# Order of a tile's interleaved Strassen units, its x sums and one h sum, in a fused attention and SiLU MLP kernel

## Chip, cores, metric

The kernel runs on one core of a Trainium2 chip. The metric is the device time of one launch in microseconds (us), the median of several runs; lower is better.

## The reference

Eight batches of eight heads of attention, 576 queries by 64, with keys and values averaged over groups of eight (72 pooled rows), then an MLP without bias on all 4608 tokens:

```python
k_p = k.reshape(B, H, Sp, 8, D).mean(axis=3)        # Sp = 72
v_p = v.reshape(B, H, Sp, 8, D).mean(axis=3)
scores = np.matmul(q, k_p.transpose(0, 1, 3, 2)) / np.sqrt(D)
attn = np.exp(scores - scores.max(-1, keepdims=True)); attn /= attn.sum(-1, keepdims=True)
x = np.matmul(attn, v_p).transpose(0, 2, 1, 3).reshape(4608, 512)
h = x @ w_in                                        # 512 -> 2048
out = (h * sigmoid(h)) @ w_out                      # 2048 -> 512
```

## The kernel before, in words

**Tiles and stages.** The 4608 tokens are cut into nine tiles of 512, numbered 0 to 8 (`NT = 9`, `B = 8`). A tile has an *up* stage (`up`: h = silu(x @ w_in), written to `h_T` as 16 groups of 128 hidden columns) and a *down* stage (`down_quarters`: h @ w_out). While tile t runs, the attention of batch t + 1 is computed between its matmuls; it writes x, transposed, to `xT`. For tiles 7 and 8 there is no attention left to put in.

**Units.** A part of each stage is done by Strassen's scheme: the two operands are cut into 2 by 2 quarters, and seven products of quarter sums take the place of eight. In `up`, a unit covers four groups of hidden columns: unit B the groups 4 to 7, C 8 to 11, A 12 to 15. Its products are numbered 1 to 7, each of four matmuls of 256 columns. Product 2 opens the PSUM bank P, 5 opens Q, 1 opens R; 4 and 7 are added onto P, 3 and 6 onto Q. The readers of these banks use one buffer each, shared by all units: after 2, ScalarE copies P to `r_sb` (L504); after 5, VectorE adds Q and `r_sb` into `rr_sb` (L507); after 1, VectorE forms `t_sb` (L510); after 4 and 3, ScalarE takes the SiLU of P and Q (L495); after 7 and 6, VectorE adds `t_sb` to P and Q into `c_sb` 0 and 1 (L519, L522), of which `h` and `s` take the SiLU on ScalarE. Groups 0 to 3 are plain products of four matmuls of 512 columns (`plain`, L547), with a SiLU each (L553); they are called g0 to g3 below.

**Order of tiles 7 and 8.** It is written out by hand in the two strings of `THREE`, one for each tile: `A4` is product 4 of unit A, `Ah` its first SiLU, `g1` plain group 1. The engines execute in program order.

**Sums.** Five of the seven products of a unit take a sum or difference of two x quarters, `x_sum` (`unit_x_sum`, L454, on VectorE), made once for a tile and used by its three units. In the same way the down stage's products 2, 5, 1, 7 and 6 take sums of `h_T` quarters, `h_sum` (`hidden_sum`, L615, on VectorE), made in halves of 1024 columns (7 in one piece of 2048).

**When sums are issued.** `up` and `down_quarters` walk through numbered steps (58 in the up stage of tiles 7 and 8, one per plain matmul and two per product; 112 in a down stage, one per matmul). A list of fillers holds pairs of a step and a function; `spread` issues a filler after the matmul of its step. Two fillers of one list with one step keep the order in which they were added. So a step number is a place in the program and sets the order on each engine, not a time.

In the down stage of tile 6 the fillers at steps 97 and 101 multiply the numerators of batch 7 (second and third visit, 192 columns each) into `xT` (L403); the filler at 103 makes tile 7's x sums. Tile 7 reads the first 64 tokens of batch 7 and so only its first visit, written at step 56.

**Down stage.** Product order is 2 and 5 (second halves of the contraction first), 1, 4, 3, 7, 6, in the banks P, Q, R, with readers L668 to L690. In the last tile, 8, products 1 to 6 are done first for 128 tokens of each half (steps 32 to 71), then for the other 128 (steps 72 to 111), so that stores start earlier; there L677 (copy of P after product 4) and L682 (copy of Q after product 3) are VectorE copies. Product 6 of the first pass takes steps 64 to 71. Product 7 is added onto P after L677 has read it, and 6 onto Q after L682 has read it.

```python
for n in (2, 5):
    h_at = {B - 1: 54, B: 50}.get(t, 36 if t > 1 else 45)
    f_up.append((h_at, lambda n=n: hidden_sum(n, 4, 8)))
...
product(3, 0, KQ, cc)
nc.vector.tensor_copy(out=o_sb[0][:, cs, HI], in_=ps["Q"][:, cs])
```

Of the kernel before, what the change touches and what calls it, by code (L numbers as in the profile page):

```python
# [36 lines left out]
def kernel(  # L37
# [11 lines left out]
    B, H, S, D = q.shape  # L49
# [274 lines left out]
    def part(g, f):  # L324
        return ((g, f * QF, (f + 1) * QF),)
# [36 lines left out]
    def denominators(b, segs, on_dve=False):  # L362
        st = batches[b]
        w = width(segs)
        es = st["es", segs]
        den_ps = ps_tile([128, 512], FP32, "at", "den_ps")
        for s in range(4):
            nc.tensor.matmul(  # L368
                den_ps[32 * s : 32 * (s + 1), :w],
                lhsT=ones, rhs=es[:, s, :], start=True, stop=True,  # L370
            )
        rec = mid.tile([128, VW], FP32, tag="rec", bufs=4, name="rec")[:, :w]
        if on_dve:
            nc.vector.reciprocal(rec, den_ps[:, :w])
        else:
            lnd = mid.tile([128, VW], FP32, tag="lnd", name="lnd")[:, :w]
            nc.scalar.activation(lnd, den_ps[:, :w], func=AF.Ln)  # L377
            nc.scalar.activation(rec, lnd, func=AF.Exp, scale=-1.0)
        st["rec", segs] = rec

    def numerators(b, segs, tags=("at", "at")):
        st = batches[b]
        w = width(segs)
        g0, i0, i1 = segs[0]
        c0 = b * S % NX + i0 * QP
        cols = slice(c0, c0 + (i1 - i0) * QP)
        es = st.pop(("es", segs))
        rec = st.pop(("rec", segs))
        nu = []
        for c in range(2):  # L390
            nu_ps = ps_tile([128, 512], FP32, tags[c], "nu_ps")
            for g, _, _, cs in seg_cols(segs):
                for s in range(4):
                    nc.tensor.matmul(  # L394
                        nu_ps[32 * s : 32 * (s + 1), cs],
                        lhsT=st["vp"][:, 4 * g + s, c::2],
                        rhs=es[:, s, cs],
                        start=True, stop=True,
                    )
            nu.append(nu_ps)  # L400
        ng = len(segs)
        for c in range(2):
            nc.vector.tensor_mul(  # L403
                out=xT[:, 2 * g0 + c : 2 * (g0 + ng - 1) + c + 1 : 2, cols],
                in0=nu[c][:, :w].rearrange("r (g n) -> r g n", g=ng),
                in1=rec.rearrange("r (g n) -> r g n", g=ng),
            )
# [33 lines left out]
    def x_quarter(t, i, j):  # L441
        c0 = (t * NTT + j * NQ) % NX
        return xT[:, 2 * i : 2 * i + 2, c0 : c0 + NQ]
# [8 lines left out]
    def unit_x_sum(t, n):  # L452
        a, b = U_X[n]
        nc.vector.tensor_tensor(  # L454
            out=x_sum[:, U_XI[n]], in0=x_quarter(t, *a), in1=x_quarter(t, *b),
            op=ALU.subtract if n in (3, 4) else ALU.add,
        )
# [143 lines left out]
    def quarter(i, j, ks):  # L601
        return h_T[:, j * KQ + ks.start : j * KQ + ks.stop, i * NQ : (i + 1) * NQ]
# [9 lines left out]
    def hidden_sum(n, k0, k1):  # L612
        a, b, op = H_SUMS[n]
        ks = slice(k0, k1)
        nc.vector.tensor_tensor(  # L615
            out=h_sum[n][:, ks, :], in0=quarter(*a, ks), in1=quarter(*b, ks), op=op
        )
# [175 lines left out]
    def load_half_2(name, half):  # L793
# [1 line left out]
            load_slots(nc.gpsimd, 2, name, i0, i1, half)  # L795

    THREE = (
        "g0 A2 A5 g1 A4 B2 A3 A1 B5 A7 C2 A6 B4 B3 B1 C5 Ah B7 As C4 Bh B6 C1 C3 C7 Bs"
        " g2 C6 Ch Cs g3",
        "A2 A5 g0 A4 B2 A3 A1 B5 A7 C2 A6 B4 B3 B1 C5 Ah B7 As C4 Bh B6 C1 C3 C7 Bs g1"  # L800
        " C6 Ch Cs g2 g3",
    )
# [1 line left out]
    for t in range(NT):  # L804
        a = t + 1
        f_up, f_down = [], []
        if t == 0:
            GA = 11
            items = [(g, 0, HS) for g in range(GA)]
            items += [(g, HS, NTT - HS) for g in range(GA)]  # L810
            items += [(g, 0, NTT) for g in range(GA, KG)]
            f_up += [(1, lambda: denominators(0, part(0, 1), on_dve=True))]
            f_up += [(5, lambda: denominators(0, part(1, 1), on_dve=True))]
            f_up += [(13, lambda: numerators(0, part(0, 1)))]
            f_up += [(17, lambda: numerators(0, part(1, 1)))]
        else:
            G = lambda *gs: [(g, 0, NTT) for g in gs]
            if t == 1:
                items = (
                    G(12, 13, 14, 15) + [(0, "251")] + G(8) + [(0, "43")] + G(9)  # L820
                    + [(0, "7h6")] + G(10) + [(0, "s")] + G(11, 0, 1, 2, 3)
                )
            elif t >= B - 1:
                items = []
                for it in THREE[t - B + 1].split():
                    items += [(("BCA".index(it[0])), it[1])] if it[0] in "ABC" else G(int(it[1]))
            else:
                items = (
                    G(12, 13) + [(0, "251")] + G(14) + [(0, "43")] + G(15) + [(0, "76")]
                    + [(1, "2")] + [(0, "hs")] + [(1, "51")] + G(0) + [(1, "43")] + G(1)  # L830
                    + [(1, "7h6")] + G(2) + [(1, "s")] + G(3)
                )
            if t < B - 1:
                for n in U_X:
                    f_up.append((0, lambda n=n: unit_x_sum(t, n)))
# [3 lines that stand above are left out]
            f_up.append((56, lambda: hidden_sum(6, 4, 8)))  # L839
            for n, k0 in ((2, 0), (5, 0), (1, 4), (1, 0)):  # L840
                f_up.append((64, lambda n=n, k0=k0: hidden_sum(n, k0, k0 + 4)))
            f_down.append((33, lambda: hidden_sum(7, 0, 8)))
            f_down.append((71, lambda: hidden_sum(6, 0, 4)))

        for n, t0, f_to, at, parts in (
            (1, 0, f_down, 48, (0, PW)), (3, 0, f_down, 52, (0, PW)),
# [61 lines left out]
                    f_down.append((nu_at[n], lambda: numerators(a - 1, visits[2])))  # L908
        if t in (B - 2, B - 1):
            for n in (4, 1, 3, 7, 6):  # L910
                f_down.append((103 if t < B - 1 else 44, lambda n=n: unit_x_sum(t + 1, n)))
        if t == B - 2:
            k_w = big.tile([128, 4, 2, 256], BF16, tag="k_raw2", name="w_sum12")
            v_w = big.tile([128, 4, 2, 256], BF16, tag="v_raw2", name="w_sum12")
# [37 lines left out]
```

The softmax here doesn't subtract the row's maximum and nothing guards it: scores larger than these inputs give would overflow.

## Time and profile before

| what | us |
|---|---|
| median of 5 runs (lowest, highest) | 284.66 (284.32, 284.85) |
| the profiled execution's own time | 284.85 |
| its span in the profile | 283.0 |
| around the span | 1.85 |
| TensorE matmul busy | 276.5 (98%) |
| VectorE busy | 232.3 (82%) |
| ScalarE busy | 184.5 (65%) |
| up stage of tile 7, first matmul to first matmul of its down stage | 228.92 to 242.30 |
| down stage of tile 7 | 242.30 to 254.66 |
| up stage of tile 8 | 254.66 to 267.28 |
| down stage of tile 8, to the end of the last VectorE addition | 267.28 to 280.32 |

Busy time counts a matmul from its start to its modelled end, so successive matmuls overlap by some 0.16 us; stage lengths are taken between starts. The rest of the span after 280.32 is the last store. PE is TensorE's matmuls, PEld its weight loads, DVE is VectorE, ACT ScalarE, SP and POOL the two other queues. "Chain" is the chain of waits that ended last, followed back from the last instruction.

### The profile page before, as it was taken

The numbers are of one execution on the slowest core, as the hardware profiler recorded it, in microseconds if no ns is written. First come the engines' busy times: TensorE is split into PE (matmuls) and PEld (weight loads), VectorE is DVE, ScalarE is ACT, GpSimd is POOL, SyncE is SP. The second block draws the span as 40 slices with busy tenths as digits, with TensorE's granted clock in tenths as the row PEclk, the third lists the DMA queues.
The fourth block names the chain that finished last, engine by engine and source line by source line (L and its number), as shares of the span: only waits on it lengthen the run. The fifth ranks groups of instructions, "written<-read, shape, count | busy, mean of one in ns | idle before, by whom it ended". The sixth has DMA issues, their size and how long they took to land.

```text
span 283.0 us, 6989 instructions
## 1 busy us (share of the span) xinstructions
PE 276.5 (98%) x2823; PEld 198.2 (70%) x2823; DVE 232.3 (82%) x418; ACT 184.5 (65%) x361; POOL 61.4 (22%) x79
## 2 busy tenths in 40 slices
PE   8889999999999999999999999999999999999995
PEld 5348544456777677767888776687667778688784
DVE  4887846899978898879896998799888978966973
ACT  1677766568567876687668857885779477326800
POOL 8655216332140214021402130441100000000001
PEclk9999999999999999999999999999999999999999
DMA  7999999896749863995498439597830032004104
GB/s 216 273 262 231 213 309 169 220 182 118 144 55 202 163 139 50 188 204 109 77 194 178 89 82 179 138 142 110 131 104 0 2 94 56 2 0 123 29 2 148
DMA packets 31312, 37.70 MB, mean 133 GB/s; under 512 B 10352, under 2 KB 22256, under 8 KB 31280
## 3 DMA queue, kind: packets, MB, share of 16 engines
q0 software_dynamic: 23920, 27.03, 53.2%
q1 hardware_dynamic: 6928, 9.58, 12.2%
q10 hardware_dynamic: 432, 0.66, 0.8%
q8 instruction: 22, 0.36, 0.5%
q14 instruction: 10, 0.08, 0.1%
HBM read 36.70 MB, written 9.44 MB: 163 GB/s over the span
## 4 chain that ended last, share of the span: by engine, by line
PE 90%; DVE 5%; DMA 2%; ACT 1%; issue 1%; DVEq 0%
PE hp_ps L547 23%; PE o_psP L655 15%; PE o_psQ L655 15%; PE u_psP L487 7%; PE u_psQ L487 7%; PE o_psR L655 5%; PE sc_ps L350 4%; PE o_ps L582 3%; PE nu_ps L394 3%; PE u_psR L487 2%; PE den_ps L368 2%; DMA raw<-in_k_dram 2%; PE warm_ps L704 1%; DVE w_sum L633 1%; ACT es L358 1%
## 5 line engine op out<-in xcount | busy, mean ns | idle before, releaser
L547 PE MATMUL hp_ps<-xT,w_in_sb 128*128 128x512 bf16 (+3 forms) x380 | 74.7, 337 | 0.1
L655 PEld LDWEIGHTS <-h_sum 128*128 128x128 bf16 x640 | 60.5, 98 | 12.8 <-DVE h_sum L615 1.9
L553 ACT ACTIVATE h_T<-hp_ps 128x512 bf16<-128x512 f32 (+2 forms) x87 | 46.5, 541 | 19.0 <-PE hp_ps L547 16.9
L615 DVE TENSOR_TENSOR h_sum<-h_T 128x1024 bf16<-128x1024 bf16 (+1 forms) x72 | 50.5, 742 | 5.0 <-ACT h_T L553 5.0
L547 PEld LDWEIGHTS <-w_in_sb 128*128 128x128 bf16 x380 | 36.2, 98 | 21.6 <-issue 0.6
L358 ACT ACTIVATE es<-sc_ps 72x384 bf16<-72x384 f32 (+1 forms) x100 | 38.9, 468 | 10.3 <-PE sc_ps L350 10.2
L487 PEld LDWEIGHTS <-w_sum 128*128 128x128 bf16 x340 | 33.3, 98 | 7.5
L655 PEld LDWEIGHTS <-h_T 128*128 128x128 bf16 x256 | 24.1, 98 | 4.4 <-issue 0.9
L403 DVE TENSOR_TENSOR xT<-nu_ps,rec 128x384 bf16<-128x384 f32 (+1 forms) x50 | 23.9, 530 | 0.2
L495 ACT ACTIVATE h_T<-c_sb 128x512 bf16<-128x512 f32 x34 | 20.6, 626 | 5.2 <-DVE c_sb L519 5.0
L377 ACT ACTIVATE lnd<-den_ps 128x384 f32<-128x384 f32 (+1 forms) x23 | 11.1, 484 | 19.4 <-PE den_ps L368 19.4
L158 DVE STREAM_TRANSPOSE qT<-q_bf 128x576 bf16<-128x576 bf16 x32 | 23.0, 753 | 0.6 <-DMA q_bf<-in_q_dram 0.6
L273 DVE TENSOR_TENSOR raw<-raw 128x384 f32<-128x384 f32 (+3 forms) x20 | 12.3, 616 | 7.6 <-DMA raw<-in_v_dram 4.5
L182 POOL DMA_DIRECT2D raw<-in_k_dram x5 | 7.1, 1429 | 52.5 <-DMA raw<-in_k_dram 52.5
L655 PE MATMUL o_psP<-w_out_sb,h_sum 128*128 128x256 bf16 x128 | 17.7, 273 | 0.6 <-DVE h_sum L615 0.6
L559 POOL DMA_DIRECT2D out_dram<-o_sb x2 | 1.2, 591 | 78.5 <-issue 77.6
L655 PE MATMUL o_psQ<-w_sum,h_sum 128*128 128x256 bf16 x128 | 16.7, 273 | 0.0
L655 PE MATMUL o_psQ<-w_out_sb,h_sum 128*128 128x256 bf16 x128 | 16.6, 273 | 0.0
L504 ACT COPY r_sb<-u_psP 128x512 f32<-128x512 f32 x17 | 9.9, 584 | 10.2 <-PE u_psP L487 7.6
L510 DVE TENSOR_TENSOR t_sb<-u_psR,rr_sb 128x512 f32<-128x512 f32 x17 | 11.8, 692 | 5.8 <-PE u_psR L487 4.1
L655 PE MATMUL o_psQ<-w_sum,h_T 128*128 128x256 bf16 x128 | 16.5, 273 | 0.0
L655 PE MATMUL o_psP<-w_sum,h_T 128*128 128x256 bf16 x128 | 16.5, 273 | 0.0
(83 smaller groups left out, 466.2 us busy)
## 6 DMA issues: line engine op xcount, KB each, us to landing
out_dram<-o_sb SPq DMA_DIRECT2D x128, 64.0 KB, 4.5
raw<-in_k_dram POOLq DMA_DIRECT2D x10, 576.0 KB, 9.7
raw<-in_v_dram POOLq DMA_DIRECT2D x10, 576.0 KB, 8.3
q_bf<-in_q_dram POOLq DMA_DIRECT2D x6, 576.0 KB, 13.3
w_in_sb<-in_moe_w_in_dram POOLq DMA_DIRECT2D x8, 256.0 KB, 8.3
w_out_sb<-in_moe_w_out_dram POOLq DMA_DIRECT2D x4, 512.0 KB, 13.5
raw<-in_v_dram POOLq DMA_DIRECT2D x2, 768.0 KB, 11.4
raw<-in_k_dram POOLq DMA_DIRECT2D x1, 768.0 KB, 10.1
```

The source lines that it names most:

```text
L158: nc.vector.transpose(out=st["qT"][:, a, f * QF : (f + 1) * QF].rearrange("r i c p -> r (i c p)"), in_=st["q_bf"][:, a, f * n : (f + 1) * n],)
L273: nc.vector.tensor_add(out=raw[..., :w], in0=raw[..., :w], in1=raw[..., w : 2 * w])
L350: nc.tensor.matmul(sc[s][:, cs], lhsT=kz[b % 2][rows, g, c, :], rhs=st["qT"][rows, g, i0:i1, c, :], start=(c == 0), stop=(c == 1),)
L358: nc.scalar.activation(es[:, s, :], sc[s], func=AF.Exp, scale=score_scale)
L403: nc.vector.tensor_mul(out=xT[:, 2 * g0 + c : 2 * (g0 + ng - 1) + c + 1 : 2, cols], in0=nu[c][:, :w].rearrange("r (g n) -> r g n", g=ng), ...
L487: nc.tensor.matmul(ps[y, bank][:, u, :], lhsT=w[:, kk, 128 * u : 128 * (u + 1)], rhs=x[:, kk, :], start=first and u == 0 and kk == 0, stop ...
L495: nc.scalar.activation(h_T[:, g : g + 2, j * NQ : (j + 1) * NQ], src, func=AF.Silu)
L510: tt(out=t_sb, in0=ps[y, "R"], in1=rr_sb, op=ALU.subtract)
L547: nc.tensor.matmul(hp_ps[:, r0:r1], lhsT=w_in_sb[:, kk, g * 128 : (g + 1) * 128], rhs=xT[:, kk, x0 : x0 + r1 - r0], start=(kk == 0), stop= ...
L553: nc.scalar.activation(h_T[:, g, n0 : n0 + n], hp_ps[:, :n], func=AF.Silu)
L615: nc.vector.tensor_tensor(out=h_sum[n][:, ks, :], in0=quarter(*a, ks), in1=quarter(*b, ks), op=op)
L655: nc.tensor.matmul(ps[b][:, c, :], lhsT=left(n, kt, c), rhs=W_OUT[n][:, kt, :], start=b not in begun, stop=kt == k1 - 1, skip_group_check= ...
```

## The change

Three edits to the order of instructions.

```diff
     THREE = (
-        "g0 A2 A5 g1 A4 B2 A3 A1 B5 A7 C2 A6 B4 B3 B1 C5 Ah B7 As C4 Bh B6 C1 C3 C7 Bs"
-        " g2 C6 Ch Cs g3",
+        "A2 A5 g0 B2 A4 A1 A3 B5 C2 A7 B4 A6 Ah B1 B3 As C5 B7 C4 B6 Bh C1 C3 C7 Bs g1"
+        " C6 Ch Cs g2 g3",
         "A2 A5 g0 A4 B2 A3 A1 B5 A7 C2 A6 B4 B3 B1 C5 Ah B7 As C4 Bh B6 C1 C3 C7 Bs g1"
         " C6 Ch Cs g2 g3",
     )
...
-            f_down.append((71, lambda: hidden_sum(6, 0, 4)))
+            f_down.append((71 if t < B else 50, lambda: hidden_sum(6, 0, 4)))
...
         if t in (B - 2, B - 1):
             for n in (4, 1, 3, 7, 6):
-                f_down.append((103 if t < B - 1 else 44, lambda n=n: unit_x_sum(t + 1, n)))
+                f_down.append((98 if t < B - 1 else 44, lambda n=n: unit_x_sum(t + 1, n)))
```

1. **Order of tile 7.** One plain group instead of two lies near the beginning, behind A5; g1 stands before C6, and g2 and g3 behind it (before: g3 alone). B2 moves ahead of A4, A1 ahead of A3, C2 ahead of A7, B4 ahead of A6. The string of tile 8 stays.
2. **x sums of tile 7.** The five L454 go from step 103 to 98 of tile 6's down stage. On VectorE they now stand between the two L403 of step 97 and the two of step 101, where they stood behind all four.
3. **One h sum of tile 8.** `hidden_sum(6, 0, 4)` goes from step 71 to 50 of the down stage. On VectorE it now stands between L677 and L682 of the first pass, where it stood behind L690. Before, the first pass's product 6 stands ahead of this sum in the program, so the first four of its eight blocks take what tile 7 left in that buffer; with the change it stands behind the sum and waits for it.

TensorE's and VectorE's instructions are the same in number and shape; the SP and POOL queues keep their order.

## The prediction

> **What bounds the kernel now.** I begin with the page's chain that ended last, by engine:
>
> ```profile
> PE 90%; DVE 5%; DMA 2%; ACT 1%; issue 1%; DVEq 0%
> ```
>
> TensorE sets the end, so an edit pays only where TensorE stands still. The change touches tile 7's up stage and the last down stage. Busy time by stage, tile 7's up stage above tile 8's (columns: us, then PE, PEld, DVE, ACT, POOL busy):
>
> ```profile
> 228.92:242.30 13.38, 12.79 (x102) 9.69 (x100) 10.75 (x20) 9.94 (x20) 0.00 (x0) 1.00 0.26 64
> 254.66:267.28 12.62, 12.62 (x102) 9.79 (x100) 9.38 (x15) 9.43 (x18) 0.00 (x0) 1.00 0.34 85
> ```
>
> Both hold the same 100 matmuls. Tile 8 has no idle TensorE; tile 7 takes 0.76 more. The timeline of TensorE shows where: tile 7's end, then tile 8's.
>
> ```profile
> 240.25 0.60 PE L487 MATMUL u_psQ<-x_sum,w_sum 128*128 128x256 bf16 x4
> 240.68 1.03 PE L547 MATMUL hp_ps<-xT,w_in_sb 128*128 128x512 bf16 x4
> 242.30 1.05 PE L655 MATMUL o_psP<-w_out_sb,h_sum 128*128 128x256 bf16 x8 [0.59 <-DVE h_sum L615]
> ...
> 265.12 0.60 PE L487 MATMUL u_psQ<-x_sum,w_sum 128*128 128x256 bf16 x4
> 265.55 1.89 PE L547 MATMUL hp_ps<-xT,w_in_sb 128*128 128x512 bf16 x8
> 267.28 1.04 PE L655 MATMUL o_psP<-w_out_sb,h_sum 128*128 128x256 bf16 x8
> ```
>
> Tile 7 has one plain group (0.87 from start to start) behind product C6, tile 8 has two. The chain of waits says what is late:
>
> ```profile
> 240.96 0.69 DVE c_sb L522
> 241.65 0.61 DVE h_sum L615
> 242.25 0.05 issue
> 242.30 1.05 PE o_psP L655 x8
> 243.35 0.87 PE o_psQ L655 x8
> 244.22 0.93 PE o_psP L655 x8
> 245.15 0.87 PE o_psQ L655 x8
> 246.03 1.81 PE o_psR L655 x16
> ```
>
> The first h sum stands behind C6's addition on VectorE, and one plain group doesn't cover addition and sum. Two later blocks run 0.06 long each (0.93 against 0.87; 1.81 against 1.75), for their h sums come in the same late row of seven.
>
> **The skill.** The Trainium skill's "Perfetto Trace Analysis" (Optimization Strategy) says to look for the gaps on the limiting engine and for what releases them; the 0.59 above is one. "TensorE: Matmul & The Clock Gate" (Part 3, The mechanism) has matmuls start and end strictly in order: a product that waits holds all behind it, and here o_psQ at 243.19 did wait behind o_psP. "VectorE: DVE Perf Modes" (The perf-mode tier table) gives tensor_tensor twice the rate on bf16 in SBUF as with a PSUM operand; the trace agrees, 1024 columns of L615 taking 0.68 and 512 of L522 0.69. So moved instructions keep these durations.
>
> **Part 1, the order of tile 7.** I lay the new string on TensorE from 228.92 with the trace's spacings: a product 0.437, a plain group 0.87, results 0.16 after the next start.
> - A2 228.92, A5 229.36, g0 229.79, B2 230.66, A4 231.10, A1 231.53, A3 231.97, B5 232.40, C2 232.84, A7 233.28, B4 233.71, A6 234.15, B1 234.59, B3 235.02, C5 235.46, B7 235.90, C4 236.33, B6 236.77, C1 237.21, C3 237.64, C7 238.08, g1 238.52, C6 239.39, g2 239.83, g3 240.70, down stage 241.57.
>
> Then I ask each waiting product for its releaser. The tight one is A3, which is added onto bank Q after L507 has read it. VectorE is full at that time:
>
> ```profile
> 226.79 2.07 DVE L403 TENSOR_TENSOR xT<-nu_ps,rec 128x384 bf16<-128x384 f32 x4
> 228.79 1.75 DVE L454 TENSOR_TENSOR x_sum<-xT 128x512 bf16<-128x512 bf16 x5
> 230.46 0.68 DVE L690 TENSOR_TENSOR o_sb<-o_psQ,t_sb 128x512 f32<-128x512 f32 x1
> 231.09 0.69 DVE L507 TENSOR_TENSOR rr_sb<-u_psQ,r_sb 128x512 f32<-128x512 f32 x1
> ```
>
> A5 comes 0.86 earlier than now, but L507 can't: it stays at 231.09 to 231.78 behind L690. A3 at 231.97 clears it by 0.19, of which a hand-off takes 0.05. The new order buys this by B2 and A1 ahead of A3: in tile 8's order A3 would stand at 231.53. Behind L507, ScalarE's copy for B2 runs 231.83 to 232.41, then the SiLUs of A4 (to 232.9) and A3 (to 233.4); A7 at 233.28 and A6 at 234.15 need these. From there I walk VectorE: t of A 232.17, rr of B 233.04, c of A7 233.92 and A6 234.79, t of B 235.57, rr of C 236.35, c of B7 236.97 and B6 237.57, t of C 238.35, c of C7 239.18, c of C6 240.09. Each is ahead of the product that needs it; C6 itself at 239.39 needs the SiLU of C3, which ends by 238.9. The first h sum follows at 240.70 and ends at 241.38, ahead of 241.57. Its lead over the down stage is 0.87; tile 8 has 0.85 (266.43 to 267.28) and no gap.
>
> So the down stage starts at 241.57 instead of 242.30: −0.73. The two late blocks have their sums 0.87 ahead instead of 0.74: −0.12 for both. The bounds: no gain if L507 and what follows keeps the old pace, −0.88 at most.
>
> Hidden work: ScalarE's SiLU of g3 ends near 242.3, and the third h sum behind it isn't wanted before 242.5 (VectorE is at the first three until then). What is late next is this SiLU, by a margin of 0.2.
>
> **Part 2, the x sums.** Five L454, 1.75 together, pass two L403, 1.0 together. Their first reader A4 is at 231.10; in the old place they end by 230.54, in the new by 229.6. No reader gains. The L403 passed end near 230.6 instead of 228.86: they free the banks of B5 (232.40) and C2 (232.84; A5 and B2 take the banks of the two L403 ahead) and write `xT` columns that only tile 8 reads. L690 behind both stays. I cost it at 0; bounds −0.05 and, if the slack of 1.8 at B5 were gone, a few tenths. No DMA is issued by any of the three edits.
>
> **Part 3, the h sum of tile 8.** In the last down stage VectorE reads
>
> ```profile
> 273.12 0.41 DVE L677 COPY o_sb<-o_psP 128x256 f32<-128x256 f32 x1
> 273.61 0.42 DVE L682 COPY o_sb<-o_psQ 128x256 f32<-128x256 f32 x1
> 274.66 0.42 DVE L686 TENSOR_TENSOR o_sb<-o_psP,t_sb 128x256 f32<-128x256 f32 x1 [0.62 <-PE o_psP L655]
> 275.53 0.42 DVE L690 TENSOR_TENSOR o_sb<-o_psQ,t_sb 128x256 f32<-128x256 f32 x1 [0.45 <-PE o_psQ L655]
> 275.87 0.68 DVE L615 TENSOR_TENSOR h_sum<-h_T 128x1024 bf16<-128x1024 bf16 x1
> ```
>
> The sum, 0.61 net of overlap, now starts at 273.45, and L682 at 274.06, ending at 274.48. Product 6, now at 274.46, is added onto the bank that L682 reads: it starts at 274.54. That is +0.08, and it reaches the end, for the chain there is TensorE without a gap. L686 at 274.66 isn't pushed. Taking the sum away from 275.87 gives nothing, as L674 behind it writes for readers at 279.02. Bounds: 0 (copy and sum overlap more) and +0.25 (sum and copy each restart cold).
>
> **Sum:** −0.73 − 0.12 + 0 + 0.08 = −0.77. From the profiled execution, 284.85 (span 283.0 and 1.85 around it), that makes 284.08; the median of the runs shown is 0.19 lower, so the median to expect is **283.9**.
>
> **Rivals.**
> - *The gap moves (within 0.2%).* L507 is pinned at 231.09 by VectorE's load; if the chain from there to C6's addition again takes what it takes now (231.09 to 241.65), the h sum ends at 242.25 again and only +0.08 remains: 284.7. Half of it gives 284.3. For it: the pinned start, and single `r_sb`, `rr_sb`, `t_sb`. Against: the old chain waited 1.7 and 0.35 for products of bank R that now come earlier.
> - *Slower.* The filler g1 is gone from the start, so TensorE's queue meets VectorE's load unprotected: if each unit's turn through the single buffers (3.05 to 3.26 from one L507 to the next in tile 8) grew by 0.5, A3, B3 and C3 would hold all behind them, 1.5 together: 283.9 + 1.5 = 285.4. It decides from 1.34 in all (0.77 + 0.57). Against: one serial turn of copy and four VectorE operations is 0.58 + 4 × 0.69 with hand-offs, about 3.7, and three of them from 230.5 end at 241.6, hardly later than now.
> - *Only the tail counts.* If x sums or h sum cost the upper bounds while the gap closes, −0.85 + 0.25 + 0.3 = −0.3: 284.4.
>
> **Chances.** What a measurement here can tell from no change is about 0.2%, 0.57 us. The forecast, a closed gap with 0.6 to 0.9 gained: 0.75 (faster). The gap moved by half or wholly: 0.14; the dear tail: 0.05; both stay within 0.57, so 0.19 for no change. Slower: 0.06. The range: the unknown costs make 283.8 to 284.1 of the main case; the runs' own scatter of 0.2 widens it to 283.5, and the half-moved gap carries it to 284.4.
>
> **What would show it.** Right: tile 7's up stage of 12.6 to 12.7 between starts, no wait for h_sum at its end, L507 of unit A still near 2.2 after the stage's start, L682 starting right behind the moved L615 and product 6 some 0.1 later. Wrong: idle TensorE ahead of A3, A7 or B3 with releaser L507 or L495, or a wait for h_sum that is still above 0.3.

## Result and profile after

The median fell from 284.68 to 283.97 us. The ratio is 0.9974 with a 95% interval of 0.9968 to 0.9980, which is 0.74 us less (0.57 to 0.91; the medians differ by 0.71), against 0.77 in the sum of the prediction, whose time was 283.9. One execution of the kernel before and one of e3_one_behind, of 1576 and 982 us, are slow ones that the ratios below leave out.

The changed kernel's page has this line for its chain by engine:

```profile
PE 80%; DMA 15%; DVE 2%; issue 1%; POOL 1%; POOLq 0%
```

The DMA share is not new waiting behind the change: this execution's chain is followed back through loads of the first 47 us, where before it ran through matmuls. The code is the same there, and in e1_order_alone, which has the same order of tile 7, the chain runs through matmuls again. What comes ahead of tile 7 lasts differently from one execution to another: tile 7 starts at 228.48 here, at 228.92 before, and between 228.28 and 229.26 in all eleven profiled executions, a spread larger than the gain. So stages are compared from start to start, and the whole by the medians.

The busy time by stage of the changed kernel, tile 7's up and down stages, then tile 8's up stage (columns as above):

```profile
228.48:241.10 12.62, 12.62 (x102) 9.78 (x100) 10.87 (x19) 9.68 (x19) 0.00 (x0) 1.00 0.27 68
241.10:253.35 12.25, 12.25 (x114) 10.84 (x113) 9.53 (x17) 3.33 (x5) 0.00 (x0) 1.00 0.01 1
253.35:265.97 12.62, 12.62 (x102) 9.79 (x100) 9.38 (x15) 9.43 (x18) 0.00 (x0) 1.00 0.34 85
```

Tile 7's up stage now lasts what tile 8's does, and TensorE is busy in all of it. From these windows and the timelines:

| from start to start, us | before | after | difference |
|---|---|---|---|
| up stage of tile 7 | 13.38 | 12.62 | −0.76 |
| down stage of tile 7 | 12.36 | 12.25 | −0.11 |
| up stage of tile 8 | 12.62 | 12.62 | 0 |
| last down stage, first to last block of eight matmuls | 11.54 | 11.60 | +0.06 |
| sum | | | −0.81 |

The chain of waits at the end of tile 7, where the old one went through C6's addition and the h sum:

```profile
239.10 0.44 PE u_psQ L487 x4
239.54 1.73 PE hp_ps L547 x8
241.27 0.87 PE o_psP L655 x8
242.14 0.87 PE o_psQ L655 x8
243.01 0.87 PE o_psP L655 x8
243.89 0.87 PE o_psQ L655 x8
244.76 1.77 PE o_psR L655 x16
```

C6 is followed by two plain groups and directly by the down stage. No VectorE step is left in this part of the chain, and the two blocks that ran long (0.93 and 1.81) are at 0.87 and 1.77.

### The profile page after: what moved, and what is told of

It reads as the page before. It is cut to its first block, busy times and chain, and to the rows that moved or that the text cites. A ratio compares the mean times of both kernels' runs of the same rounds, so it can differ in the third digit from the quotient of the medians.

```text
span 281.7 us, 6991 instructions
## 1 busy us (share of the span) xinstructions
PE 276.5 (98%) x2823; PEld 198.2 (70%) x2823; DVE 232.4 (82%) x418; ACT 184.8 (66%) x361; POOL 61.3 (22%) x79
## 4 chain that ended last, share of the span: by engine, by line
PE 80%; DMA 15%; DVE 2%; issue 1%; POOL 1%; POOLq 0%
PE hp_ps L547 18%; PE o_psP L655 15%; PE o_psQ L655 15%; PE u_psP L487 8%; PE u_psQ L487 8%; PE o_psR L655 5%; DMA w_out_sb<-in_moe_w_out_dram 5%; DMA raw<-in_k_dram 4%; DMA q_bf<-in_q_dram 3%; PE sc_ps L350 3%; DMA raw<-in_v_dram 3%; PE u_psR L487 3%; PE nu_ps L394 2%; PE den_ps L368 2%; DVE w_sum L633 1%
## 5 line engine op out<-in xcount | busy, mean ns | idle before, releaser
L403 DVE TENSOR_TENSOR xT<-nu_ps,rec 128x384 bf16<-128x384 f32 (+1 forms) x50 | 23.9, 531 | 0.2
L507 DVE TENSOR_TENSOR rr_sb<-u_psQ,r_sb 128x512 f32<-128x512 f32 x17 | 11.7, 691 | 5.6 <-ACT r_sb L504 5.0
```

The costliest lines, as they stand in the source:

```text
L403: nc.vector.tensor_mul(out=xT[:, 2 * g0 + c : 2 * (g0 + ng - 1) + c + 1 : 2, cols], in0=nu[c][:, :w].rearrange("r (g n) -> r g n", g=ng), ...
L507: tt(out=rr_sb, in0=ps[y, "Q"], in1=r_sb, op=ALU.add)
```

## Experiments

Every kernel was profiled once and timed; stage lengths are from its timeline of TensorE, from start to start. "Last down" runs to the start of the last block of eight matmuls. Ratios are to the kernel before, run beside each group, where its median was 284.69 (e1 to e4), 284.65 (e5 to e8) and 284.33 (e9).

| kernel | up 7 | down 7 | last down | median | ratio, 95% interval |
|---|---|---|---|---|---|
| before | 13.38 | 12.36 | 11.54 | 284.68 | |
| after | 12.62 | 12.25 | 11.60 | 283.97 | 0.9974 (0.9968 to 0.9980) |
| e1_order_alone | 12.63 | 12.24 | 11.54 | 283.76 | 0.9975 (0.9963 to 0.9987) |
| e2_hsum_alone | 13.38 | 12.35 | 11.60 | 284.76 | 1.0000 (0.9990 to 1.0011) |
| e3_one_behind | 13.38 | 12.36 | 11.60 | 284.90 | 1.0008 (0.9999 to 1.0016) |
| e4_copy_on_act | 12.62 | 12.25 | 11.38 | 283.52 | 0.9957 (0.9945 to 0.9969) |
| e5_tile8_order | 12.76 | 12.25 | 11.61 | 284.17 | 0.9985 (0.9977 to 0.9993) |
| e6_no_plain_first | 13.19 | 12.22 | 11.60 | 284.35 | 0.9990 (0.9982 to 0.9999) |
| e7_load2 | 13.23 | 12.25 | 11.60 | 284.76 | 1.0005 (0.9997 to 1.0014) |
| e8_load5 | 14.62 | 12.25 | 11.67 | 286.02 | 1.0055 (1.0038 to 1.0072) |
| e9_old_load5 | 15.14 | 12.35 | 11.54 | 286.06 | 1.0053 (1.0035 to 1.0070) |

**e1_order_alone**: part 1 without the two other edits.

```diff
 # against the changed kernel
-f_down.append((71 if t < B else 50, lambda: hidden_sum(6, 0, 4)))
+f_down.append((71, lambda: hidden_sum(6, 0, 4)))
...
-f_down.append((98 if t < B - 1 else 44, lambda n=n: unit_x_sum(t + 1, n)))
+f_down.append((103 if t < B - 1 else 44, lambda n=n: unit_x_sum(t + 1, n)))
```

> Tile 7's new string alone; x sums stay at step 103, the h sum at 71. Theory (the whole gain is the cover of two plain groups behind C6; the x sums' place is worth nothing): tile 7's up stage 12.62 between starts as in the changed kernel, its down stage 12.25, the last down stage 0.06 shorter than in the changed kernel; about 283.85 to 283.95 against 284.68. Rival (the x sums' earlier place is what lets A4 or A1 go on time): TensorE idles ahead of A4 or A1, the up stage is 12.8 or longer, and less than 0.6 us is gained.

The up and down stages are those of the changed kernel within 0.01, and the last down stage is back at 11.54. So the order of tile 7 makes the whole gain, and the place of the x sums adds no time to it. (The x sums' move was not run alone; this is read from the up stages with and without it, 12.62 and 12.63.)

**e2_hsum_alone**: part 3 alone.

```diff
 # against the kernel before
-f_down.append((71, lambda: hidden_sum(6, 0, 4)))
+f_down.append((71 if t < B else 50, lambda: hidden_sum(6, 0, 4)))
```

> The h sum of tile 8 at step 50 alone, all else as before. Theory: L682 starts 0.3 later behind the moved L615, the first pass's product 6 0.06 to 0.08 late, nothing given back at step 71: +0.06 us, which the timing alone can't tell from zero but the timeline can. Rival (the sum costs as much as its own time, or taking it from step 71 pays it back): +0.2 or more, or 0.0 in the stage from 267.28 to the last addition (13.04).

The stage is 0.06 longer, as in the changed kernel; the timing can't tell that from nothing. Nothing comes back from step 71. What part 3 buys is the operand of that product 6, not time.

**e3_one_behind**: the new string, but with g2 ahead of C6.

```diff
 # against the changed kernel, the end of tile 7's string
-... C1 C3 C7 Bs g1 C6 Ch Cs g2 g3
+... C1 C3 C7 Bs g1 g2 C6 Ch Cs g3
```

> The changed kernel with g2 back in front of C6, so that one plain group stands behind C6 as before, while B2 and A1 keep their new places. Theory (the cover behind C6 is what pays): the gap in front of the down stage returns with releaser h_sum, about 0.75 between starts, the up stage is 13.4 and the down stage 12.36 again: 284.7. Rival (the earlier chain through r_sb, rr_sb and t_sb is what pays, as C6's addition no longer waits for it): the up stage stays near 12.7 to 12.9 and 0.4 us or more of the gain remains.

The gap is back to the hundredth, 13.38. First TensorE's timeline, then the waits of the weight loads:

```profile
240.17 0.60 PE L487 MATMUL u_psQ<-x_sum,w_sum 128*128 128x256 bf16 x4
240.60 1.03 PE L547 MATMUL hp_ps<-xT,w_in_sb 128*128 128x512 bf16 x4
242.22 1.05 PE L655 MATMUL o_psP<-w_out_sb,h_sum 128*128 128x256 bf16 x8 [0.59 <-ACT h_T L495]
```

```profile
PEld L655 <- DVE h_sum L615: 1.4, 3, 1.1
```

The first names ScalarE: its last SiLU of unit C ended at about the same time as the first h sum (242.23 and 242.16), and the view names what ended last. Yet that SiLU ended no sooner than the product began. The weight load of the product, which reads the h sum, names VectorE (1.1 us at most), and so does the program, in which this product doesn't wait for that SiLU. VectorE itself had stood idle 0.96 ahead of C6's addition, waiting for C6's matmuls:

```profile
240.87 0.69 DVE L522 TENSOR_TENSOR c_sb<-u_psQ,t_sb 128x512 f32<-128x512 f32 x1 [0.96 <-PE u_psQ L487]
```

So an earlier chain through the shared buffers brings nothing by itself, since the addition can't precede the product. As long as the first h sum stands behind that addition, what counts is the work behind C6 on TensorE: one plain group of 0.87 doesn't cover 0.69 and 0.61 with their hand-offs, and two, 1.73, do.

That the sum stands there is the program's order and not a dependence; neither the prediction nor its rivals go into this. It is `hidden_sum(2, 4, 8)` and reads groups 4 to 7 and 12 to 15, units B and A, nothing of C. The last SiLU that it reads is `Bs`; in the kernel before it ended at 240.31, and C6's addition began at 240.96:

```profile
239.69 0.62 ACT L495 ACTIVATE h_T<-c_sb 128x512 bf16<-128x512 f32 x1
```

Taking this sum ahead of C6's addition on VectorE is thus a second way at the gap. No run has it. It would push back the addition, `Cs` and the later sums that read unit C, so what it would bring is open.

**e5_tile8_order**: tile 8's string for tile 7 too.

```diff
 # against the changed kernel, the beginning of tile 7's string
-A2 A5 g0 B2 A4 A1 A3 B5 C2 A7 B4 A6 Ah B1 B3 As C5 B7 C4 B6 ...
+A2 A5 g0 A4 B2 A3 A1 B5 A7 C2 A6 B4 B3 B1 C5 Ah B7 As C4 Bh B6 ...
```

> The changed kernel with tile 8's own string for tile 7 as well (A4 ahead of B2, A3 ahead of A1 and so on). Theory (the new string's only advantage over tile 8's is to put A3 0.44 later, behind L507, which VectorE's load holds): by the changed kernel's trace L507 ends 2.69 after the stage's start and A3 would come at 2.62, so A3 waits 0.1 to 0.15 with releaser rr_sb and the up stage is 12.75; about 284.1. Prediction on record had 0.3 for this. Rival (units in tile 7 run as in tile 8 whatever the start): 12.62 and no wait.

The stage is 0.14 longer: A3 starts at 232.01, 0.05 behind L507's end (231.28 + 0.68), where TensorE without a wait would have had it at 231.88. So B2 and A1 ahead of A3 are worth 0.14 and two plain groups behind C6 the rest.

**e6_no_plain_first**: g0 at the end as well.

```diff
 # against the changed kernel
-A2 A5 g0 B2 A4 ... Ch Cs g2 g3
+A2 A5 B2 A4 ... Ch Cs g0 g2 g3
```

> The changed kernel with g0 moved from behind A5 to the end, ahead of g2: no plain group at the beginning, three behind C6. Theory (A3 can't pass the end of L507, 2.69 after the stage's start): A3 would stand at 2.18 and waits 0.56; the cover behind C6 grows by 0.87 for nothing; up stage 13.2, about 284.5. Rival (the larger lead at the end absorbs a stall at the beginning): 12.6 to 12.8.

Measured 13.19 for 13.2. The stall stands where it was expected, and the third group of cover gives none of it back in this stage (0.03 in the next):

```profile
231.49 0.60 PE L487 MATMUL u_psQ<-x_sum,w_in_sb 128*128 128x256 bf16 x4 [0.40 <-DVE rr_sb L507]
```

**e7_load2 and e8_load5**: more work on VectorE at the beginning of tile 7 (two and five more sums).

```diff
 # against the changed kernel; range(5) in e8_load5
+if t == B - 2:
+    for _ in range(2):
+        f_down.append((98, lambda: unit_x_sum(t + 1, 6)))
```

> The changed kernel with two more x sums (n = 6 again, into the same buffer with the same values) behind the five: 0.70 more on VectorE at the beginning of tile 7. Theory: L507 of unit A ends 0.70 later, of which 0.31 is slack, so A3 waits 0.39 and the up stage is 13.0; about 284.35. Rival (the new order protects the beginning of the tile): no wait, 283.97.

> As the last, with five more x sums: 1.75 more on VectorE. Theory: A3 waits 1.75 - 0.31 = 1.44, the up stage is 14.05, about 285.4, slower than before: the slower rival of the prediction with its cause put in by hand. Rival (the two plain groups at the end take part of the stall up, since the h sums' lead grows): under 1.0, and no slower than before.

Both cost more than expected, 0.61 and 2.00 in the stage for 0.39 and 1.44. The timeline of VectorE of e7_load2, then of e8_load5, and A3's line of TensorE's in each:

```profile
227.29 2.67 DVE L454 TENSOR_TENSOR x_sum<-xT 128x512 bf16<-128x512 bf16 x7
231.42 0.68 DVE L507 TENSOR_TENSOR rr_sb<-u_psQ,r_sb 128x512 f32<-128x512 f32 x1
```

```profile
227.09 4.06 DVE L454 TENSOR_TENSOR x_sum<-xT 128x512 bf16<-128x512 bf16 x10
232.60 0.68 DVE L507 TENSOR_TENSOR rr_sb<-u_psQ,r_sb 128x512 f32<-128x512 f32 x1
```

```profile
232.15 0.60 PE L487 MATMUL u_psQ<-x_sum,w_in_sb 128*128 128x256 bf16 x4 [0.45 <-DVE rr_sb L507]
```

```profile
233.33 0.60 PE L487 MATMUL u_psQ<-x_sum,w_in_sb 128*128 128x256 bf16 x4 [1.84 <-DVE rr_sb L507]
```

The wrong term of the expectation was the price of an added sum. Five take 1.75, seven 2.67, ten 4.06: an added one costs 0.46, not 0.35. With 0.92 and 2.31 put on VectorE the slack of 0.31 gives 0.61 and 2.00, which is what was measured. A3 starts 0.05 behind L507's end in both (232.10 and 233.28). e8_load5 shows that enough load on VectorE makes the new order slower, here by 0.38% to 0.72%. It does so through one stall at A3 and none at B3 or C3; the prediction's slower rival, in which every unit's turn grows, was not put in. In this one execution tile 8's stages are also 0.13 longer in all, behind a VectorE addition that began 0.35 late there; why is open.

**e9_old_load5**: the five sums added to the kernel before, at its step 103.

> The kernel before with the same five more x sums at the beginning of tile 7. An added sum costs 0.46 on VectorE (measured: 2.31 for five), so L507 ends at 4.89 + 0.29 = 5.17 after the stage's start. Theory (the old order's A3, at 3.48 after the start, has a slack of 0.57 behind L507 where the new one has 0.31, for g1 stands ahead of it): A3 waits 2.31 - 0.57 = 1.74 with releaser rr_sb, the gap ahead of the down stage stays, the up stage is 13.38 + 1.74 = 15.1, about 286.4. Rival (the gap at the end and the stall at the beginning are one wait seen twice): the up stage is near 14.6, as with the new order.

The old order waits twice:

```profile
228.68 0.81 PE L547 MATMUL hp_ps<-xT,w_in_sb 128*128 128x512 bf16 x3
229.33 0.60 PE L487 MATMUL u_psP<-xT,w_sum 128*128 128x256 bf16 x4
233.70 0.60 PE L487 MATMUL u_psQ<-x_sum,w_in_sb 128*128 128x256 bf16 x4 [1.59 <-DVE rr_sb L507]
243.60 1.05 PE L655 MATMUL o_psP<-w_out_sb,h_sum 128*128 128x256 bf16 x8 [0.59 <-DVE h_sum L615]
```

The first line needs care. It has three of g0's four matmuls: the record of the first is missing from this trace. A2 stands 0.87 behind the stage's start in the kernel before, so the stage starts at 229.33 − 0.87 = 228.46; g0's four weight loads are all there, the first at 228.36, 0.10 ahead of its matmul as in the kernel before. From 228.46 the up stage is 15.14. A3 stands 5.24 behind the start, where the kernel before has it at 3.48: a stall of 1.76, for 1.74 expected, again 0.05 behind L507's end.

The stall at A3 and the gap at the end are two waits: 13.38 + 1.76 = 15.14. The rival of one wait seen twice, 14.6, falls. From the start to the last block this execution is 1.76 longer than the kernel before, and its median 1.73. The new order's lead in the up stage shrinks under this load from 0.76 to 0.52 (15.14 − 14.62), about the 0.26 by which its A3 has less slack (0.31 for 0.57).

**e4_copy_on_act**: a version that may beat both.

```diff
 # against the changed kernel, down_quarters
-copy = nc.vector.tensor_copy if last else nc.scalar.copy
+copy = nc.vector.tensor_copy if last and cc == (1,) else nc.scalar.copy
```

> The changed kernel with the copy of P after product 4 in the first pass of the last down stage (L677) on ScalarE, which is idle there, in place of VectorE. Theory (in this stage VectorE's row h_sum 7, L674, L677, h_sum 6, L682 makes product 7 wait 0.18 for L677 and product 6 0.06 for L682): both waits go, the last down stage is 0.2 to 0.24 shorter, about 283.75. Rival (the copy on ScalarE takes 0.58 or more instead of 0.42 and ends no earlier, or the wait moves to L686): less than 0.1 us, below nothing if ScalarE waits for stores.

The chain of the first pass in the changed kernel, with both waits, and then in e4_copy_on_act. A block of eight that waits for nothing takes 0.87; products 7 and 6 take 1.04 (with the 0.01) and 0.93 in the first:

```profile
271.39 0.87 PE o_psQ L655 x8
272.27 0.01 issue
272.28 1.03 PE o_psP L655 x8
273.31 0.93 PE o_psQ L655 x8
```

```profile
271.80 0.87 PE o_psQ L655 x8
272.67 0.87 PE o_psP L655 x8
273.54 0.87 PE o_psQ L655 x8
```

ScalarE's copy takes 0.37:

```profile
271.83 0.37 ACT L677 COPY o_sb<-o_psP 128x256 f32<-128x256 f32 x1 [2.00 <-PE o_psP L655]
```

Both waits are gone, 0.22 of the stage, and the rival's price of 0.58 was too high: that is the copy of twice the columns. Its ratio to the kernel before, 0.9957 (0.9945 to 0.9969), lies clear of 1. That it beats the changed kernel is shown by the stage alone: the two were not timed beside each other, and their intervals overlap.

## Why the prediction was right

- **The gap at the end of tile 7** was forecast as −0.73 from the laid-out string, with −0.12 for two late blocks. Measured: −0.76 and −0.11. e3_one_behind shows the cause by undoing only that. The walk along VectorE held too: each operation from L507 to C6's addition starts within 0.16 of where it was put, counted from the stage's start, and C6's addition to the hundredth, at 11.17:

```profile
239.65 0.69 DVE L522 TENSOR_TENSOR c_sb<-u_psQ,t_sb 128x512 f32<-128x512 f32 x1
240.26 4.29 DVE L615 TENSOR_TENSOR h_sum<-h_T 128x1024 bf16<-128x1024 bf16 x7
```

The first of these seven sums takes 0.68 and ends at 240.94, 0.16 ahead of the down stage, for 0.19 worked out. So the gap is closed, but with little to spare. The prediction's next late thing, the SiLU of g3, has less margin than it said: it ends at 241.98, and the first sum behind it, the fourth and not the third, starts at 242.06, 0.08 later for 0.2.
- **A3 behind L507** was named as the tight place, with a slack of 0.19. Here are VectorE and then A3 in the changed kernel:

```profile
226.35 1.02 DVE L403 TENSOR_TENSOR xT<-nu_ps,rec 128x384 bf16<-128x384 f32 x2
227.29 1.75 DVE L454 TENSOR_TENSOR x_sum<-xT 128x512 bf16<-128x512 bf16 x5
228.96 1.01 DVE L403 TENSOR_TENSOR xT<-nu_ps,rec 128x384 bf16<-128x384 f32 x2
229.90 0.68 DVE L690 TENSOR_TENSOR o_sb<-o_psQ,t_sb 128x512 f32<-128x512 f32 x1
230.49 0.68 DVE L507 TENSOR_TENSOR rr_sb<-u_psQ,r_sb 128x512 f32<-128x512 f32 x1
```

```profile
231.53 0.60 PE L487 MATMUL u_psQ<-x_sum,w_in_sb 128*128 128x256 bf16 x4
```

L507 starts 2.01 after the stage's start, for 2.17 worked out, so A3 has 0.36 behind L507's end, 0.31 of it slack after the hand-off. In e1_order_alone, with the x sums behind all four L403, L507 starts at 2.14. The move of part 2 therefore brings 0.13 of slack, no time; the prediction had costed it at nothing. Why is argued, not shown by a run: the second pair of L403 had to wait a little for its matmuls, and the x sums now fill that wait. The trace of the kernel before fits this, for its four L403 start 0.48, 0.58 and 0.48 apart, the long step ahead of the second pair.
- **The tail** was forecast at +0.08, measured at +0.06, and by the mechanism named:

```profile
271.81 0.41 DVE L677 COPY o_sb<-o_psP 128x256 f32<-128x256 f32 x1
272.14 0.68 DVE L615 TENSOR_TENSOR h_sum<-h_T 128x1024 bf16<-128x1024 bf16 x1
272.74 0.42 DVE L682 COPY o_sb<-o_psQ 128x256 f32<-128x256 f32 x1
```

L682 starts directly behind the moved sum and ends at 273.16; product 6 starts 0.05 later.
- **The rivals.** The gap moved nowhere. The slower case needs 1.34 of stalls and there were none; it takes the load of e8_load5 to make the new order slower, and then by one stall and not by three. Of the dear tail, 0.25 and 0.3, the h sum cost 0.06 and the x sums nothing. e5_tile8_order shows one smaller slip: the prediction's times put A3 in tile 8's order 0.25 ahead of L507's end (231.53 against 231.78), a stall of 0.3 with the hand-off; 0.14 was measured, since L507 is earlier.
- **Where luck comes in.** No term of the sum is off by more than 0.03, and that is read from stages. That the total by the timing, 0.74, is as near to 0.77 is more than the timing can vouch for: its interval is 0.34 wide.

## What to carry to other kernels

At the end of a stage, ask how much matmul work stands behind the last product whose result other engines handle ahead of what the next stage waits for. If it is less than that path, move independent work there; in this kernel an earlier chain ahead of that product brought nothing. Ask too whether the next stage needs that result at all, or only stands behind it in a queue: then the queue's order is a second place to look. Fillers at a stage's beginning are worth only the stall they cover: here one plain group was enough behind A5, and a reader's slack behind a loaded engine says in advance how many can be taken away. A sum put into an engine's queue costs what it delays there, not its own length: here 0.06 for 0.6. And before a stage's length is taken from a trace, count the matmuls of its first row.

## What the runs showed of the hardware that was not expected

- An x sum added behind five others, into the same part of the same buffer as the last of them, cost 0.46 us where the five are 0.33 apart (1.75 for five, 2.67 for seven, 4.06 for ten). One sum is recorded with 0.42. In e8_load5's trace each added sum carries a wait on VectorE's own semaphore, which the sum ahead of it raises, and starts 0.03 behind that one's recorded end; the third to fifth carry no wait, and start 0.08 ahead of it. No run has sums of the same output without the wait.
- ScalarE copied 256 columns from PSUM in 0.37 us (L677 in e4_copy_on_act) and VectorE in 0.41 (L677 in the changed kernel), while at 512 columns, in earlier tiles, ScalarE took 0.59 (L677) and VectorE 0.69 (L682): here ScalarE was the quicker of the two at both sizes.
